# The second half of the last reload in four parts of rows, and a late correction moved from TensorE to VectorE

## The chip, the cores and the metric

The kernel runs on one core of a Trainium2 chip. The metric is the device time of one execution in microseconds (us), taken as the median of several timed runs. The profile comes from one further execution that the hardware profiler recorded.

## What is computed

The input `u` has 2048 tokens of 512 channels. A layer norm without weights gives `xn`. Two branches use it, and their results are added to the input:

```python
xn = (u - mean(u)) / sqrt(var(u) + 1e-5)                 # over the 512 channels
K  = Re(sum over 128 modes of C * exp(dt*A*l) * (dt*B))  # a filter of length 2048 for each channel
y  = irfft(rfft(pad(xn)) * rfft(pad(K)))[:2048] + xn * Dskip
h  = sigmoid(xn @ w_gate) * (xn @ w_up)                  # 512 -> 1792
out = u + y + h @ w_down                                 # 1792 -> 512
```

## The kernel before

**The two branches.** The gated branch runs in four groups of 512 tokens (`grp` 0 to 3). For each of 14 slices of 128 hidden columns TensorE computes the gate (L1045) and the up product (L1069), four matmuls each; ScalarE makes the sigmoid (L1057, L1060) and, for most slices, a copy of the up product (L1084); VectorE multiplies (L1089 from the copy, L1094 from PSUM). The down product (L1123) takes 14 matmuls of 512 columns for each tile of 128 tokens. The convolution branch is a Fourier transform over the tokens written as matmuls. It runs in two halves of 256 channels (`p` 0 and 1) with eight units `u` each. A unit transforms a slice (L885), brings the filter's spectrum to the same layout (L911), multiplies on VectorE (L916, L920), goes half the way back (L935), is copied to SBUF by ScalarE (L288) and stored to a scratch tensor `v_scr` in DRAM (L942). The last step of the way back mixes all units, so V is read again with the partition axis rearranged, and then multiplied with the constant `S2` (L994 in `s2_mm`).

**The reload.** `reload()` (L972) reads V back. The first half of the channels (`p` 0, `v0`) is four loads over all 128 partitions. The second half (`p` 1, `vall`) is cut by `VPART` (L409) into a part with six of the units, rows 0 to 95 of the scratch and partitions 32 to 127 of SBUF, and a part with the two units that are stored last, partitions 0 to 31. Each part is four loads `k`, one for each group of four output tiles, and each row of a load is two pieces of 2 KB (one for each `j`). `vall` has the order `[j, tile, channel]`.

**The tail.** Twelve of the sixteen output tiles have their gated result ready in SBUF early (`glu_sb`, with the input already added). For them `final(t)` (L999) runs `s2_mm` for a pair of tiles into one of two PSUM pairs, eight matmuls, and VectorE adds the gated result and writes the output tile (L1020, 1024 columns). The four tiles of group 3, tiles 12 to 15, are "late": TensorE sums the down product and the S2 product in one PSUM bank, and VectorE adds the input `xt` (L1143). The last of these is done in two halves of 256 columns. `xt` is a second load of tiles 12 to 15 of the input, issued on SP's queue late in the kernel (L1110), since the first copy was overwritten by the layer norm.

**The correction.** The way the input is laid out leaves out a few terms of the convolution for the last rows. Eight rows of corrections are computed from the first tokens (`pre`, L714) and two filter taps (`k2`, L950): five small VectorE operations make `rz` (L954 to L958), TensorE transposes it into PSUM (L964), ScalarE copies it to `rr` (L966), and in `s2_mm` one more matmul for each late tile (L997, 512 columns, or 256 in the halves) adds the right row through the selector `SR` (a constant, loaded at L852). `rr` is set to zero first by GpSimd (L854).

**What sets the order.** All work is recorded as operations of a `_Plan`. `ORDER` (L206) is a list of operation numbers, written out by hand, and the program is emitted in that order; so each engine's instruction order and each queue's order of DMAs is fixed. The slots of PSUM and of SBUF buffers are taken and returned in that same order. Most DMAs go through SP's queue, a few through ScalarE's and GpSimd's. The DMAs of SP and ScalarE take turns on eight semaphores, DMAHW0 to 7, so the issue of a DMA also waits until the DMA that had its semaphore before has landed.

Of the kernel before, what the change touches and what calls it, by code (L numbers as in the profile page):

```python
# [20 lines left out]
D = 512  # L21
# [38 lines left out]
PK = [42.24, 48.91]  # L60
SWD = (4, 6, 7)
# [121 lines left out]
def _consts():  # L183
# [16 lines left out]
    return dict(SR=f(sr), ident=f(np.eye(128)), S1=f(np.tile(S1, (4, 1))), S2=f(np.stack([_build_S2(by), np.roll(_build_S2(by), 32, axis=1)], axis=1)), M2=f(quads(M2[by])),  # L200
                MAB=f(np.stack([quads(MA[by], True), quads(MB[by], True)], axis=2)), E=f(_build_E(M2, by).reshape(128, NU // 2, 2, NKT, 128).transpose(1, 0, 2, 3, 4)))
# [117 lines left out]
def kernel(  # L319
# [75 lines left out]
    for nm, sz in [("W1", 12 * KB), ("gc", 2 * KB), ("G", 16 * KB), ("H", 20992), ("tmp", 4 * KB), ("W0", 12 * KB),  # L395
                   ("xn", 16 * KB), ("lad", 16 * KB), ("kx", 8 * KB), ("zs", 4 * KB), ("pq", 2 * KB)]:
        OFF[nm] = o
        o += sz
    s1 = at(OFF["kx"], [64])
    s2 = at(OFF["tmp"], [2, 64])  # L400
    rr = at(OFF["tmp"] + KB // 2, [D])
    sr = at(OFF["tmp"] + 3 * KB // 2, [4, 64])
    W = [at(OFF["W%d" % p], [12, 2, DW]) for p in range(NP)]
# [809 lines left out]
```

## Time and profile before

| | |
|---|---|
| three timed runs | 214.19, 215.49, 216.25 us; median 215.49 |
| profiled execution, its span from the first to the last instruction (no other time of it is given) | 213.6 us |
| TensorE (PE) busy | 204.2 us, 96% |
| VectorE (DVE) busy | 191.3 us, 90% |
| ScalarE (ACT) busy | 177.1 us, 83% |
| GpSimd (POOL) busy | 27.8 us, 13% |
| granted TensorE clock, mean | 1.000 |
| moved by DMA | 42.61 MB, mean 199 GB/s |

The rows that the prediction quotes are of these kinds. A row of the timeline has the start in us, the duration in us, the engine, the line, the operation, the tiles as out<-in, the shape, the count of merged instructions, and in brackets the idle time before it with what ended it. A name such as SPq is the sequencer of an engine that issues DMAs. A row of the windows has, for a stretch of time, the busy us and the number of instructions of PE, PEld (weight loads), DVE, ACT and POOL, then the granted clock, the mean busy share of the 16 DMA engines and what they moved in GB/s. Consecutive TensorE matmuls overlap, so the time that one costs is the distance between starts, which is shorter than its duration.

### The profile page before, as it was taken

The page shows a single profiled execution, that of the slowest core. Times are in us where ns is not written, and L with a number is a line of the kernel's source. Part 1 is how long each engine was busy: PE and PEld are TensorE (multiplying, and loading weights), DVE is VectorE, ACT ScalarE, POOL GpSimd, SP SyncE. Part 2 cuts the span into 40 slices and gives each one's busy share as a digit, 9 for nine tenths or more (in the row PEclk, how much of TensorE's full clock was granted, in tenths as well). Part 3 has the DMA queues.
Part 4 walks back from the last instruction along what each step waited for, and adds up shares of the span by engine and source line. Part 5 has one row for each costly group of instructions (what it writes and reads, how often), then busy time and mean ns, then how long its engine had stood idle before and what let it go on. Part 6 is the DMA issues. An engine that isn't in the chain of part 4 may idle for free.

```text
span 213.6 us, 4875 instructions
## 1 busy us (share of the span) xinstructions
PE 204.2 (96%) x1838; PEld 102.9 (48%) x1864; DVE 191.3 (90%) x406; ACT 177.1 (83%) x284; POOL 27.8 (13%) x32
## 2 busy tenths in 40 slices
PE   7989999999999999999999999999999999999992
PEld 2654444444443444445436555544654645644482
DVE  4799999999979999999999999999992999990494
ACT  5699999999999999997999989978989998870000
POOL 2120026008980000002000000001200000000000
PEclk9999999999999999999999999999999999999999
DMA  5999269124464236967965878787967799698864
GB/s 148 316 383 381 100 147 324 61 98 147 110 126 104 76 105 229 213 191 151 249 185 141 228 202 237 215 221 175 202 188 208 217 284 274 141 357 218 240 213 172
DMA packets 52377, 42.61 MB, mean 199 GB/s; under 512 B 16641, under 2 KB 44546, under 8 KB 52354
## 3 DMA queue, kind: packets, MB, share of 16 engines
q1 hardware_dynamic: 50658, 40.30, 63.9%
q0 software_dynamic: 864, 1.57, 4.8%
q10 hardware_dynamic: 832, 0.43, 0.8%
q8 instruction: 14, 0.23, 0.5%
q14 instruction: 9, 0.07, 0.1%
HBM read 24.99 MB, written 12.85 MB: 177 GB/s over the span
## 4 chain that ended last, share of the span: by engine, by line
PE 41%; DVE 40%; POOL 6%; DMA 4%; issue 4%; ACT 3%; DVEq 0%; SPq 0%; ACTq 0%
PE pair L911 8%; PE bank L1045 7%; PE bank L1123 7%; PE bank L1069 7%; DVE big L737 6%; DVE big L738 6%; POOL ln_ve_b L481 5%; PE pair L935 5%; DVE big L742 4%; DVE big L743 4%; DVE stats L542 3%; DVE hT_sb L1094 3%; DVE hT_sb L1089 3%; DVE big L678 2%; DMA big<-v_scr 2%
## 5 line engine op out<-in xcount | busy, mean ns | idle before, releaser
L288 ACT ACTIVATE big<-pair 128x1024 bf16<-128x1024 f32 x64 | 64.5, 1039 | 6.9 <-DVE big L920 1.7
L1069 PE MATMUL bank<-xnT,wu_sb 128*128 128x512 bf16 x214 | 52.9, 379 | 1.7 <-issue 0.6
L1123 PE MATMUL bank<-wd_sb,hT_sb 128*128 128x512 bf16 (+1 forms) x231 | 50.6, 367 | 0.5 <-issue 0.2
L1045 PE MATMUL bank<-xnT,wg_sb 128*128 128x512 bf16 (+1 forms) x191 | 45.6, 370 | 1.0 <-issue 0.5
L1045 PEld LDWEIGHTS <-wg_sb 128*128 128x128 bf16 x240 | 22.5, 98 | 25.0 <-issue 3.2
L1123 PEld LDWEIGHTS <-hT_sb 128*128 128x128 bf16 x238 | 22.4, 98 | 24.9 <-issue 1.6
L1069 PEld LDWEIGHTS <-wu_sb 128*128 128x128 bf16 x224 | 20.7, 98 | 27.5 <-issue 5.4
L1057 ACT ACTIVATE hT_sb<-bank 128x512 bf16<-128x512 f32 x48 | 28.2, 627 | 0.7 <-PE bank L1045 0.7
L737 DVE TENSOR_TENSOR big<-big 128x1024 bf16<-128x1024 bf16 (+4 forms) x40 | 26.7, 667 | 0.2
L738 DVE TENSOR_TENSOR big<-big 128x1024 bf16<-128x1024 bf16 (+4 forms) x40 | 26.5, 663 | 0.0
L1084 ACT ACTIVATE us_sb<-bank 128x512 bf16<-128x512 f32 x40 | 23.6, 616 | 0.6 <-DVE hT_sb L1089 0.3
L911 PE MATMUL pair<-big 128*128 128x256 bf16 x160 | 19.8, 273 | 0.0
L916 DVE TENSOR_TENSOR big<-big 128x2048 bf16<-128x2048 bf16 x16 | 19.3, 1217 | 0.1
L911 PEld LDWEIGHTS <-big 128*128 128x128 bf16 x160 | 15.4, 98 | 4.7 <-issue 0.8
L481 POOL TENSOR_SCALAR ln_ve_b<-mvb 128x4 bf16<-128x4 bf16 x3 | 13.0, 4323 | 34.1 <-DVE mvb L543 34.1
L742 DVE TENSOR_TENSOR big<-big 128x512 bf16<-128x512 bf16 (+4 forms) x40 | 16.5, 413 | 0.2
L743 DVE TENSOR_TENSOR big<-big 128x512 bf16<-128x512 bf16 (+4 forms) x40 | 16.5, 412 | 0.0
L792 ACT ACTIVATE sq_sb<-big 128x256 bf16<-128x256 bf16 (+2 forms) x20 | 13.2, 658 | 1.6 <-DVE big L743 1.5
L1089 DVE TENSOR_TENSOR hT_sb<-hT_sb,us_sb 128x1024 bf16<-128x1024 bf16 x20 | 13.5, 683 | 0.0
L935 PE MATMUL pair<-big 64*64 64x512 bf16 (+1 forms) x256 | 13.1, 327 | 0.0
L898 DVE COPY big<-big 32x1024 bf16<-32x1024 bf16 x20 | 8.4, 418 | 4.5 <-ACT big L288 4.2
L288 ACT ACTIVATE big<-big 128x256 bf16<-128x256 bf16 x30 | 12.4, 452 | 0.0
(99 smaller groups left out, 229.8 us busy)
## 6 DMA issues: line engine op xcount, KB each, us to landing
big<-c_E SPq DMA_DIRECT2D x13, 320.0 KB, 4.4
z_scr<-big SPq DMA_DIRECT2D x16, 256.0 KB, 2.9
big<-z_scr SPq DMA_DIRECT2D x16, 256.0 KB, 4.2
v_scr<-big SPq DMA_DIRECT2D x16, 256.0 KB, 3.2
big<-big SPq DMA_DIRECT2D x44, 64.0 KB, 3.3
big<-in_A_u_dram SPq DMA_DIRECT2D x4, 512.0 KB, 9.1
wu_sb<-in_B_w_up_dram SPq DMA_DIRECT2D x2, 896.0 KB, 10.8
wd_sb<-in_B_w_down_dram SPq DMA_DIRECT2D x1, 1792.0 KB, 9.0
```

Source lines behind the costliest of these rows:

```text
L288: nc.scalar.activation(out=get(out), in_=get(in_), func=ACT.Identity)
L481: P.tensor_scalar(out=q["ve_b"], in0=mvb[:, s, 1], scalar1=EPS, scalar2=None, op0=ALU.add)
L737: V.tensor_tensor(out=wide(outp), in0=wide(lo), in1=mre, op=ALU.mult)
L738: V.tensor_tensor(out=wide(tb()), in0=wide(lo), in1=mim, op=ALU.mult)
L742: V.tensor_tensor(out=outp[:, :, 0], in0=outp[:, :, 0], in1=tb()[:, :, 1], op=opr)
L743: V.tensor_tensor(out=outp[:, :, 1], in0=outp[:, :, 1], in1=tb()[:, :, 0], op=opi)
L911: T.matmul(two(sk)[:, o:o + DW], es()[:, g, kt, :], kTv[p][:, :, kt, :], start=kt in (0, NKT - 1), stop=kt >= NKT - 2)
L935: T.matmul(two(sv)[o:o + 64, DW * (2 * g + y):2 * DW * (g + 1)], mab[b:b + 64, 2 * u + g, q, :], pq()[b:b + 64, q, ch] if y else pp()[b:b ...
L1045: T.matmul(bank(sl, k % 2)[:, c0:c1], w[:, kt, k * 128:(k + 1) * 128], xnT[:, grp, kt, c0:c1], start=(kt == 0), stop=(kt == KT - 1))
L1057: S.activation(out=hT_sb[:, hs.idx, k % 2, :], in_=bank(sl), func=ACT.Sigmoid)
L1069: T.matmul(bank(sl), wu_sb[:, kt, k * 128:(k + 1) * 128], xnT[:, grp, kt, :], start=(kt == 0), stop=(kt == KT - 1))
L1123: T.matmul(bank(po)[:, 0:c[1] - c[0]], hT_sb[:, hts[k // 2].idx, k % 2, jj * 128:(jj + 1) * 128], wd_sb[:, k, c[0]:c[1]], start=first and ...
```

## The change

1. **The second half in four parts.** `VPART` cuts the second half by units 2-3, 4-5, 6-7 and 0-1. Each part has 32 rows, and these no longer go to neighbouring partitions: row `a` of part `b` goes to partition `4a + b`, so each part touches every fourth partition from end to end. The S2 constant for the second half has its rows rearranged to match, so `S2` is 64 KB, not 32.
2. **Longer pieces.** Columns of the constant `MAB` are reordered so that a row of V in the scratch has the order `[tile group, j, tile, channel]`, with tile groups in the order 0, 3, 1, 2 (`KORD`). The first three parts are then two loads each with one piece of 8 KB per row (256 KB a load; the first has tile groups 0 and 3, the second 1 and 2), and the last part is four loads with 4 KB pieces (128 KB each), two of them on ScalarE's queue as before. The loads of the first half have one piece of 4 KB per row.
3. **The last x tiles are kept.** Tiles 12 to 15 of the input are loaded to a tile `xt` of their own at the start, the layer norm reads them there and writes to `xn`, and the second load of 512 KB is gone.
4. **The correction on VectorE.** Two loads of 4 KB bring the eight input rows concerned next to the correction (`x8`). In the place of ScalarE's copy, VectorE adds the transposed correction to them (8x512), and two DMAs on ScalarE's queue write the eight sums over rows 95 and 127 of `xt`. The matmuls of L997, the load of `SR` (64 KB) and GpSimd's memset are gone.
5. **The order.** `ORDER` is new near the end.

```diff
-    sr = np.zeros((128, 4, 64))
-    for q in range(8):
-        sr[q, q // 2, 31 + 32 * ((q ^ (q // 2)) % 2)] = 1.0
...
+    MAB = MAB.reshape(MAB.shape[:3] + (2, 2, 4, 4)).swapaxes(4, 5)[..., KORD, :, :].reshape(MAB.shape)
+    spread = S2.reshape(4, 32, -1).swapaxes(0, 1)
...
-    VPART = ((0, 0, 8, 4), (1, 2, 8, 4), (1, 0, 2, 4))
+    VPART = ((0, 0, 8, 4), (1, 2, 4, 2), (1, 4, 6, 2), (1, 6, 8, 2), (1, 0, 2, 4))
...
-        ls = [load("SP", xn[:, i0:i0 + n, :], xv[:, i0:i0 + n, :], 128 * n * KB,
+        ls = [load("SP", xt[:] if i0 == 12 else xn[:, i0:i0 + n, :], xv[:, i0:i0 + n, :], 128 * n * KB,
...
-    l_sr = load("SP", sr, cten["SR"].ap(), 64 * KB, deps=table_free, pkt=512)
-    l_s2 = load("SP", s2, cten["S2"].ap(), 32 * KB, deps=table_free, pkt=256)
-    m_rr = pl.add("POOL", 0.3, lambda: P.memset(rr, 0.0), table_free, 60)
+    l_x8 = [load("SP", x8[b:8:2, :], xv[95 + 32 * b, 12:16, :], 4 * KB, deps=table_free, pkt=1024) for b in range(2)]
+    l_s2 = load("SP", s2, cten["S2"].ap(), 64 * KB, deps=table_free, pkt=512)
...
-    o_rz = pl.add("ACT", 0.48, lambda slr=slr: S.activation(out=rr[0:8, :], in_=bank(slr)[0:8, :], func=ACT.Identity), [o_rt, l_sr, m_rr], 60, rel=[slr])
-
-    vall = at(TAIL["vall"] + 16 * KB, [2, NT, DW])
+    o_rz = pl.add("DVE", 0.61, lambda slr=slr: V.tensor_tensor(out=rr[0:8, :], in0=bank(slr)[0:8, :], in1=x8[0:8, :], op=ALU.add), [o_rt] + l_x8, 60, rel=[slr])
+
+    vall = at(TAIL["vall"] + 16 * KB, [4, 2, 4, DW])
+    vspread = vall.rearrange("(a b) k j i d -> b a (k j i d)", b=4)
...
-                dst = v0[k][rows] if p == 0 else vall[rows, :, w * k:w * (k + 1)]
...
+                ks = KORD[w // 4 * k:w // 4 * (k + 1)]
+                cut = slice(2 * DW * w * k, 2 * DW * w * (k + 1))
+                dst = vspread[u0 // 2][:, cut] if p else v0[ks[0]].rearrange("p j i d -> p (j i d)")
...
-        if i >= 12:
-            T.matmul(o[64:128, :], sr[:, i - 12, :], rr[:, w[0]:w[1]], start=False, tile_position=(0, 64), **kw)
...
-                    xt = at(TAIL["xt"], [4, D])
-                    lx = [dma("SP", xt, xv[:, i:i + 4, :], deps=[prods[0]] + table_free, prio=3,
-                              pkt=4096)(512 * KB)]
+                    lx = [dma("ACT", xt[95 + 32 * b:96 + 32 * b, :, :], rr[b:8:2, :], deps=xn_ready[12:16] + [o_rz], prio=3, pkt=1024)(4 * KB) for b in range(2)]
...
-            ver = vp_op[i // 2] + [l_s2, o_rz]
+            ver = vp_op[i // 2] + [l_s2]
```

What the new order makes of the engines near the end is shown at three places. In these rows `pair_63` and `pair_64` are the two PSUM pairs, `bank_65` to `bank_68` the four banks, `big` is the large SBUF tile that holds most buffers, and brackets name the semaphores that an instruction waits for.

TensorE after its 28th matmul of the group-3 down products (L1123; L1129 in the changed kernel), where the first S2 products stand (L994; L1004). Rows that only repeat are left out. Before:

```order
L1123 MATMUL bank_67<-wd_sb,hT_sb 128x512
L994 MATMUL pair_64<-xnT,big 64x256 [waits DMAHW5_49]
L994 LDWEIGHTS big [waits DMAHW4_49]
L994 MATMUL pair_64<-big 64x256 [waits DMAHW2_49]
L994 MATMUL pair_63<-xnT,big 64x256 [waits Activation_49]
L1123 MATMUL bank_65<-wd_sb,hT_sb 128x512
```

Changed:

```order
L1129 MATMUL bank_66<-wd_sb,hT_sb 128x512
L1004 LDWEIGHTS big [waits DMAHW4_49]
L1004 MATMUL bank_66<-big 64x256 [waits DMAHW4_49]
L1004 LDWEIGHTS big [waits DMAHW5_49,DMAHW4_49,DMAHW3_49]
L1004 MATMUL bank_66<-big 64x256 [waits DMAHW0_49]
L1004 MATMUL bank_68<-big 64x256
L1004 MATMUL pair_64<-xnT,big 64x256 [waits DMAHW6_49]
L1004 MATMUL pair_64<-big 64x256 [waits DMAHW0_49]
```

Eight S2 matmuls of the first two late tiles (banks 66 and 68) now stand ahead of the first two finals; before they stood, with a matmul of L997 each, behind the third down product in bank 65. So the first S2 matmul now needs tile group 3 of all four parts, and the finals behind it need group 0.

VectorE from its last product of the gated branch to the end. L1020 and L1143 are L1028 and L1149 in the changed kernel. Before:

```order
L1094 TENSOR_TENSOR hT_sb<-hT_sb,bank_66 128x512
L1020 TENSOR_TENSOR big<-pair_64,glu_sb 128x1024
L1020 TENSOR_TENSOR big<-pair_63,glu_sb 128x1024
L1143 TENSOR_TENSOR big<-bank_68,big 128x512
L1143 TENSOR_TENSOR big<-bank_67,big 128x512
L1143 TENSOR_TENSOR big<-bank_65,big 128x512
L1020 TENSOR_TENSOR big<-pair_64,glu_sb 128x1024
```

Changed:

```order
L1102 TENSOR_TENSOR hT_sb<-hT_sb,bank_67 128x512
L973 TENSOR_TENSOR big<-pair_63,big 8x512
L1028 TENSOR_TENSOR big<-pair_64,glu_sb 128x1024
L1028 TENSOR_TENSOR big<-pair_63,glu_sb 128x1024
L1149 TENSOR_TENSOR big<-bank_68,xt 128x512
L1149 TENSOR_TENSOR big<-bank_66,xt 128x512
L1149 TENSOR_TENSOR big<-bank_65,xt 128x512
L1028 TENSOR_TENSOR big<-pair_64,glu_sb 128x1024
```

The order of kinds is the same, and the addition of the correction (L973) has come in ahead of the first final. What differs is when the banks of the first two late tiles are ready, by the rows of TensorE above.

SP's queue around the last stores of V. Before, `v_scr_100` is the part with six units and `v_scr_101` that with the last two:

```order
L422 DMA big<-in_A_u_dram 128x2048 [waits DMAHW3_49]
L422 DMA v_scr_101<-big 128x4x256 [waits DMAHW0_49,Activation_49]
L422 DMA v_scr_101<-big 128x4x256 [waits DMAHW1_49,Activation_49]
L422 DMA big<-v_scr_100 96x2x1024 [waits DMAHW4_49,DMAHW6_49,DMAHW2_49,DVE_49]
L422 DMA big<-v_scr_101 32x2x1024 [waits DMAHW1_49,DMAHW0_49]
L422 DMA big<-v_scr_100 96x2x1024 [waits DVE_49]
```

Changed, where `v_scr_101`, `_102` and `_103` are the parts of units 2-3, 4-5 and 6-7, and `v_scr_104` that of the last two units:

```order
L430 DMA v_scr_101<-big 128x4x256 [waits DMAHW7_49,Activation_49]
L430 DMA big<-v_scr_102 32x4096 [waits DMAHW1_49,DMAHW3_49,DMAHW0_49,DVE_49]
L430 DMA v_scr_104<-big 128x4x256 [waits Activation_49]
L430 DMA v_scr_104<-big 128x4x256 [waits DMAHW2_49,Activation_49]
L430 DMA big<-v_scr_103 32x4096
L430 DMA big<-v_scr_101 32x4096 [waits DMAHW7_49,DMAHW5_49]
L430 DMA big<-v_scr_104 32x2048 [waits DMAHW2_49,DMAHW1_49,DMAHW0_49]
L430 DMA big<-v_scr_104 32x2048 [waits DVE_49]
L430 DMA big<-v_scr_102 32x4096 [waits DMAHW3_49,DVE_49]
```

One load of the second half now stands ahead of the last two stores, two stand between them and the load that waits for them, and the load of the input is gone. On ScalarE's queue stand, in this order, two loads of `v_scr_104` and the two DMAs from the correction to `xt`. On ScalarE itself two copies of the up product (L1084) now stand ahead of the copy that the sixth unit's store waits for, and on TensorE a group of four up matmuls has changed places with the four gate matmuls next to it.

More of the change, by code (lines that the diff above doesn't have):

```diff
@@ L540, in layernorm @@
                 continue
-            b_s = pl.add("DVE", 0.6, lambda i=i: V.bn_stats(out=stats[:, i, :], in_=xn[:, i, :]), l_x[i], prio)
+            b_s = pl.add("DVE", 0.6, lambda i=i: V.bn_stats(out=stats[:, i, :], in_=x_in(i)), l_x[i], prio)
             st.append(pl.add("DVE", 0.1, lambda i=i: V.bn_aggr(out=mvb[:, i, :], in_=stats[:, i, :]), [b_s], prio - 0.001))
@@ L548, in fa @@
                 def fa(i=i):
[L549 removed]
+                    S.activation(out=xn[:, i, :], in_=x_in(i), func=ACT.Identity, scale=lnt["ri_f"][:, i:i + 1],
                                  bias=lnt["nb_f"][:, i:i + 1])
@@ L973, in reload @@
         for n, (p, u0, u1, nt) in enumerate(VPART):
[L974 to L975 removed]
+            v_v = v_scr[n][:].rearrange("g q d -> (g q) d").rearrange("(p kc) d -> p (kc d)", kc=32)
             for k in range(nt):
                 w = NT // nt
[L978 to L983 removed]
+                ks = KORD[w // 4 * k:w // 4 * (k + 1)]
+                cut = slice(2 * DW * w * k, 2 * DW * w * (k + 1))
+                dst = vspread[u0 // 2][:, cut] if p else v0[ks[0]].rearrange("p j i d -> p (j i d)")
+                free = x_use[ks[0]] + ([o_pre] if ks[0] == 0 else []) if p == 0 and ks[0] < 3 else table_free if p == 0 else table_free + x_done
+                ld = dma("ACT" if n == 4 and k % 2 else "SP", dst, v_v[:, cut], deps=v_st[n] + free, prio=20 + n + 0.02 * k,
+                         pkt=1024 * w, hv=0.9)(16 * KB * w * (u1 - u0))
+                for kk in ks:
+                    vp_op[2 * kk].append(ld)
+                    vp_op[2 * kk + 1].append(ld)
     def glu_at(i):
```

38 lines of the change are left out of this document (18 added, 20 removed), and 82 rows, old and new, of the table ORDER.

## Prediction

> **What bounds the kernel now.** I read the stages first (the windows), then each engine's timeline in the last stages, then the landings of the DMAs that feed them.
>
> ```profile
> 165.00:182.00 17.00, 16.50 (x163) 9.75 (x168) 16.58 (x28) 15.43 (x18) 0.00 (x0) 1.00 0.88 252
> 182.00:192.00 10.00, 9.79 (x103) 5.33 (x98) 9.90 (x20) 7.88 (x10) 0.00 (x0) 1.00 0.82 254
> 192.00:198.10 6.10, 6.10 (x31) 2.60 (x30) 0.73 (x2) 0.59 (x1) 0.00 (x0) 1.00 0.86 228
> 198.10:202.60 4.50, 4.06 (x30) 2.07 (x30) 2.36 (x2) 0.00 (x0) 0.00 (x0) 1.00 0.84 223
> 202.60:206.90 4.30, 4.30 (x52) 3.64 (x51) 3.56 (x5) 0.00 (x0) 0.00 (x0) 1.00 0.69 233
> 206.90:210.50 3.60, 2.96 (x33) 2.11 (x30) 3.57 (x5) 0.00 (x0) 0.00 (x0) 1.00 0.62 228
> ```
>
> Up to 192 us both TensorE (9.79 of 10.00) and VectorE (9.90 of 10.00) are full: an edit there gains little unless it removes work from both. From 192 to 198.1 only TensorE works (6.10 of 6.10) and VectorE has nothing to do. From 202.6 on VectorE is nearly full again. So the tail goes from TensorE to VectorE, and the question is where it changes hands.
>
> ```profile
> 191.94 6.22 PE L1123 MATMUL bank<-wd_sb,hT_sb 128*128 128x512 bf16 x28
> 198.09 0.30 PE L994 MATMUL pair<-xnT,big 128*64 128x256 bf16 x2
> 198.67 0.30 PE L994 MATMUL pair<-big 128*64 128x256 bf16 x2 [0.28 <-DMA big<-v_scr]
> 198.80 0.28 PE L994 MATMUL pair<-xnT,big 128*64 128x256 bf16 x2
> 199.35 0.28 PE L994 MATMUL pair<-big 128*64 128x256 bf16 x2
> 199.78 2.97 PE L1123 MATMUL bank<-wd_sb,hT_sb 128*128 128x512 bf16 x13 [0.16 <-issue]
> 202.68 0.51 PE L994 MATMUL bank<-big 128*64 128x256 bf16 x5
> 205.21 0.27 PE L994 MATMUL pair<-big 128*64 128x256 bf16 x1
> 199.23 2.36 DVE L1020 TENSOR_TENSOR big<-pair,glu_sb 128x1024 bf16<-128x1024 f32 x2 [6.50 <-PE pair L994]
> 203.34 1.94 DVE L1143 TENSOR_TENSOR big<-bank,big 128x512 bf16<-128x512 f32 x3 [1.76 <-PE bank L997]
> 205.20 2.34 DVE L1020 TENSOR_TENSOR big<-pair,glu_sb 128x1024 bf16<-128x1024 f32 x2
> 207.47 0.41 DVE L1143 TENSOR_TENSOR big<-bank,big 128x256 bf16<-128x256 f32 x1
> 207.80 2.34 DVE L1020 TENSOR_TENSOR big<-pair,big 128x1024 bf16<-128x1024 f32 x2
> 210.06 0.41 DVE L1143 TENSOR_TENSOR big<-bank,big 128x256 bf16<-128x256 f32 x1
> 210.14 0.33 DVEq L1209
> ```
>
> Three things are to be seen. TensorE reaches the first S2 product at 198.09 and its second pair, due one step of 0.11 us later (198.80 to 199.35 are five steps), starts at 198.67: it lost 0.47 us to a load of V. VectorE idles 1.76 us before the first late addition at 203.34, because that tile's S2 and correction matmuls stand behind the third down product. And from 203.34 to the end at 210.47 VectorE never stops: 7.13 us, so the end is VectorE's. After that come 3.1 us of output DMA and closing, which the change leaves as they are.
>
> **The change, part by part.** *Order of the tail.* With the S2 products of late tiles 12 and 13 ahead of the finals, both banks are complete before VectorE ends its two finals. First S2 at 198.09 without a wait; four steps for the banks (0.44), then the eight steps of the two finals. The first final's last step starts at 198.09 + 7 x 0.11 = 198.86, and VectorE starts 0.32 later (199.23 less 198.91, one step after 198.80) at 199.18, as before. Two finals at 1.13 (half of 205.20 to 207.47) and two late additions at 0.62 (a third of 203.34 to 205.20) end at 202.7. The third late tile: before, its first S2 step came at 202.68, which is 4.12 after 198.09 when the 0.47 are taken out; now 198.09 + 0.44 + 4.12 = 202.65, second step 202.76, ready at 203.08. From there VectorE has one late addition, four finals and two halves, all continuous: 7.13 - 2 x 0.62 = 5.89, so it ends at 208.97 and not 210.47. **Gain 1.50 us**: 1.24 from two additions that move into the idle time, 0.26 from the block's earlier start.
>
> *The matmuls of L997.* From 202.68 to 205.21 there are 15 steps of 0.11 (1.65) and the five correction matmuls: 2.53 - 1.65 = 0.88 us of TensorE. It is not added to the sum: they stood in front of VectorE's block only through the first of them. But it is what keeps TensorE ahead afterwards. Its next steps are: two finals and the half bank from 202.87 to 203.85, 256-column down products until 205.3 (like 205.42 to 207.05), finals 205.5 to 206.5 (the second waits for its PSUM pair until about 206.0), down products until 208.2. VectorE wants those results at 203.7, 204.8, 205.9, 206.3, 207.4 and 208.6; each is there by 0.1 us or more. If this cover were gone, 0.88 would come back behind 203.08.
>
> *The loads of V.* This decides whether the 198.09 stands.
>
> ```profile
> 191.27 2.59 DMA v_scr<-big
> 193.92 4.70 DMA big<-v_scr
> big<-v_scr SPq DMA_DIRECT2D x4, 384.0 KB, 7.0
> big<-v_scr ACTq DMA_DIRECT2D x2, 128.0 KB, 5.2
> DMA to landing us min/median/max: 2.5/4.3/7.2
> big<-in_A_u_dram SPq DMA_DIRECT2D x4, 128.0 KB, 2.2
> 188.00:190.00 2.00, 2.00 (x35) 1.02 (x34) 2.00 (x5) 1.02 (x2) 0.00 (x0) 1.00 1.08 383
> 194.00:195.00 1.00, 1.00 (x7) 0.41 (x5) 0.00 (x0) 0.00 (x0) 0.00 (x0) 1.00 0.70 219
> 195.00:196.00 1.00, 1.00 (x6) 0.46 (x5) 0.00 (x0) 0.00 (x0) 0.00 (x0) 1.00 0.70 201
> ```
>
> The last store is issued at 191.27 and lands 2.59 us later, 193.86; no load of the last two units can go before, in either kernel. Before, that load took 4.70 us for 128 KB, behind 384 KB, while loads of 96 and 32 neighbouring partitions moved 201 to 219 GB/s with engines idle (share 0.70); with loads over all 128 partitions in flight the DMAs reached 383 GB/s (188 to 190). No row shows a load of 32 rows set four apart. Bounds for its landing after an issue at 193.94: 2.2 us (the row of 128 KB alone) gives 196.1; 7.2, the slowest load of V, gives 201.1. Between them: what is still to move for the first S2 step when stores end, about 193.2, is two loads of 256 KB and two of 128 KB, 786 kB, at 210 GB/s 3.7 us, so 196.9, some 197.5 with the other two 128 KB loads beside it. I take 197.2, 0.9 us before 198.09, so the wait is 0; it costs nothing only while the 28 down products (6.1 us) run over it. The later halves are issued by 197 and wanted at 202.9, with 3 us to spare even at 2.5 to 3 us each.
>
> [...]
>
> *What is removed from SP and DMA.*
>
> ```profile
> 182.41 1.42 SPq L422 DMA_DIRECT2D big<-in_A_u_dram  x1
> 190.35 1.27 SPq L422 DMA_DIRECT2D v_scr<-big  x2
> 165.21 0.55 SPq L422 DMA_DIRECT2D big<-c_SR  x1
> 165.80 1.93 SPq L422 DMA_DIRECT2D big<-big  x3
> 172.03 1.23 DVE L916 TENSOR_TENSOR big<-big 128x2048 bf16<-128x2048 bf16 x1
> ```
>
> The 512 KB input load with its 1.42 us of SP's queue goes; two loads of V's first half move up by that much, out of the way of the last stores. Nothing on the path waits there, so 0; at most the 0.21 us that TensorE is not busy between 182 and 192, and the 0.50 of the stage before. The one load of `SR` becomes two small ones, another 0.6 us of queue ahead of three swaps of a unit. The last of them was issued at about 167.1 and is read by the product at 172.03, so even with the median 3.3 us of such swaps there is room for 0.6.
>
> *VectorE and ScalarE before the tail.*
>
> ```profile
> 189.26 1.28 DVE L1089 TENSOR_TENSOR hT_sb<-hT_sb,us_sb 128x1024 bf16<-128x1024 bf16 x2
> 190.47 0.17 DVE L954 TENSOR_TENSOR rf<-pre,k 128x16 f32<-128x16 f32 x1
> 191.62 0.39 PE L964 MATMUL pair<-ident,rz 128*8 128x128 bf16 x4
> big<-big SPq DMA_DIRECT2D x44, 64.0 KB, 3.3
> ```
>
> One product of 0.60 now stands before the five small operations, which then end at about 191.6, where the transpose at 191.62 waits for them: up to 0.1 later for TensorE and all behind it; I take **0.05 loss**. The addition of the correction (8x512 from PSUM, by the nearest row 0.62) runs at about 192.8 to 193.5, in the 6.5 us that VectorE idles; without that cover it would cost 0.62. Its two DMAs to `xt` are third and fourth on ScalarE's queue, issued by 196; by 2.2 to 5.2 us they land between 198 and 201.2, and the first late addition starts at 201.4. The two copies of ScalarE that move ahead delay the sixth unit's store by 1.1 us, to about 188; it is not among the last two, and the loads of its part go after 191.6. I take 0 for both.
>
> The sum: 1.50 - 0.05 = 1.45 us. Span 213.6 becomes 212.15. The runs' median of 215.49 lies 1.9 above the span, and the same distance gives **214.0 us**, 0.7% faster. About 1% (2.15 us) is what a measurement of this kernel can tell from no change; the three runs lie 2.06 apart.
>
> **The rivals.** *Slower: the wait at the first S2 step.* This step now needs group 3 of all parts, the last of it from ScalarE's queue, and twice the bytes of the second half before it. Every us that this lands after 198.1 is added to the end. With 7.2 us it lands at 201.1: 3.0 us of wait against 1.45 of gain, 217.0 us. It decides from a landing at 199.6. For it: two landings near 7 us in the same place. Against it: those loads queued behind up to 0.9 MB, and the pending bytes are fewer now. Chance 0.12.
>
> *The wait stays as it was.* The last load takes 4.7 to 5.2 us as in the old rows and lands at 198.6 to 199.1, a wait of 0.5 to 1.0: 214.8. Chance 0.17.
>
> *The early relief counts.* The freed queue closes TensorE's gaps of 0.21 and 0.50 us: 213.3. Against it: those gaps end with "issue" or VectorE, not DMA. Chance 0.10.
>
> *The change does not do what it says.* If the eight sums reach `xt` only at about 203, behind the loads on ScalarE's queue, the first two late additions find the banks complete but not the input, and the idle time stays: 215.3. Chance 0.06.
>
> **How the numbers follow.** The forecast has 0.55. Of it 0.17 falls beyond 1% by the spread of the runs; with 0.07 of the third rival and 0.03 of the second, faster has 0.27. Of the first rival 0.06 is beyond +1% (a landing after 201.7, or 217.0 and some spread), and 0.02 of the rest: slower 0.08. The remaining 0.65 is within 1%. The range 212.3 to 216.3 reaches from 1.7 below, the spread and the third rival, to between the last rivals and the first.
>
> **What would show it.** Right: no L997; the first S2 matmul at 198.1 to 198.2 and no DMA wait in the eight steps; VectorE's two late additions start at 201.4 directly behind the two finals, with 0.3 to 0.4 of idle ahead of the third; VectorE ends near 209.0; the last 128 KB loads land in 3 to 3.5 us. Wrong: a wait for `big<-v_scr` or for `xt<-big` of over 0.5 us, VectorE idle after 203.1, or TensorE starting its 28 matmuls later than 192.1.

## The result, and the profile after

The changed kernel takes **213.69 us** (median of 20 runs, 212.38 to 214.69); the kernel before took 215.1 in 20 runs beside it (213.74 to 217.49). The ratio is 0.9933, 95% interval 0.9908 to 0.9957: 0.7% faster, within the 1% that was called no change. The forecast was 214.0 against 215.49, a ratio of 0.9931.

The stages of the changed kernel, in windows cut at its own hand-overs (first TensorE's 28 down products alone, then the tail):

```profile
182.80:192.80 10.00, 9.79 (x105) 5.31 (x98) 9.90 (x20) 7.89 (x11) 0.00 (x0) 1.00 0.78 232
192.80:198.90 6.10, 6.10 (x29) 2.62 (x28) 1.35 (x3) 0.00 (x0) 0.00 (x0) 1.00 0.87 262
198.90:203.40 4.50, 4.34 (x38) 2.52 (x38) 3.38 (x4) 0.00 (x0) 0.00 (x0) 1.00 0.61 199
203.40:207.70 4.30, 4.30 (x57) 3.47 (x57) 3.94 (x6) 0.00 (x0) 0.00 (x0) 1.00 0.55 202
207.70:209.80 2.10, 1.54 (x14) 1.13 (x12) 2.10 (x3) 0.00 (x0) 0.00 (x0) 1.00 0.76 271
```

Up to 192.8 nothing changed (TensorE 9.79 of 10.00, VectorE 9.90, as before). In the third row VectorE is busy for 3.38 us where the matching stage of before had 2.36.

The whole of this execution runs 0.83 us behind the one of before, from its start: VectorE waited about that much longer for the first input tiles, which both kernels load in the same way. The first fence is from VectorE's timeline before, the second from that of the changed kernel; the bracket is the wait for the load.

```profile
2.92 1.29 DVE L542 BATCH_NORM_STATS2 stats<-big 128x6 f32<-128x512 bf16 x2 [2.92 <-DMA big<-in_A_u_dram]
4.61 0.69 DVE L542 BATCH_NORM_STATS2 stats<-big 128x6 f32<-128x512 bf16 x1
```

```profile
3.48 1.28 DVE L550 BATCH_NORM_STATS2 stats<-big 128x6 f32<-128x512 bf16 x2 [3.48 <-DMA big<-in_A_u_dram]
5.62 0.69 DVE L550 BATCH_NORM_STATS2 stats<-big 128x6 f32<-128x512 bf16 x1 [0.36 <-DMA big<-in_A_u_dram]
```

The third tile came 1.01 us later (5.62 less 4.61), and 0.83 of it is still there at the first down product (192.77 against 191.94). The change is not the reason: in the runs below that load the input as the changed kernel does, the first down product starts anywhere from 190.82 (e10) to 192.47 (e7). So the spans (212.7 and 213.6) differ by less than the tails do. I compare **tails** from here on: from the start of the first of the 28 down products to the end of VectorE's last addition. Before, that was 191.94 to 210.47 = 18.53 us. After, from the timelines of TensorE and VectorE:

```profile
192.45 0.39 PE L971 MATMUL pair<-ident,rz 128*8 128x128 bf16 x4
192.77 6.22 PE L1129 MATMUL bank<-wd_sb,hT_sb 128*128 128x512 bf16 x28
198.91 0.63 PE L1004 MATMUL bank<-big 128*64 128x256 bf16 x8
203.47 0.41 PE L1004 MATMUL bank<-big 128*64 128x256 bf16 x4
207.54 1.70 PE L1129 MATMUL bank<-wd_sb,hT_sb 128*128 128x256 bf16 x14
193.47 0.67 DVE L973 TENSOR_TENSOR big<-pair,big 8x512 bf16<-8x512 f32 x1
200.02 2.36 DVE L1028 TENSOR_TENSOR big<-pair,glu_sb 128x1024 bf16<-128x1024 f32 x2 [5.87 <-PE pair L1004]
202.29 1.28 DVE L1149 TENSOR_TENSOR big<-bank,xt 128x512 bf16<-128x512 f32 x2
203.93 0.69 DVE L1149 TENSOR_TENSOR big<-bank,xt 128x512 bf16<-128x512 f32 x1 [0.35 <-PE bank L1004]
204.53 2.34 DVE L1028 TENSOR_TENSOR big<-pair,glu_sb 128x1024 bf16<-128x1024 f32 x2
206.79 0.41 DVE L1149 TENSOR_TENSOR big<-bank,xt 128x256 bf16<-128x256 f32 x1
207.13 2.34 DVE L1028 TENSOR_TENSOR big<-pair,big 128x1024 bf16<-128x1024 f32 x2
209.39 0.41 DVE L1149 TENSOR_TENSOR big<-bank,xt 128x256 bf16<-128x256 f32 x1
```

192.77 to 209.80 is **17.03 us, 1.50 less than before**. The eight S2 matmuls of tiles 12 and 13 start at 198.91 as one unbroken group; no wait stands in brackets. The two late additions (202.29) follow the two finals directly, where VectorE idled 1.76 us before.

TensorE waits for no load and no other engine there either. Its last down product before ended here:

```profile
208.16 1.70 PE L1123 MATMUL bank<-wd_sb,hT_sb 128*128 128x256 bf16 x14
```

That is 209.86, or 17.92 after its first; now it is 209.24, or 16.47 after. TensorE's part of the tail became 1.45 us shorter: the lost 0.47, the five matmuls' 0.88, and a rest of 0.10. VectorE's last addition follows it by 0.2 and 0.15 us in the two kernels. Two chains thus end almost together in both, and this decides the experiments.

### The profile page after: what moved, and what is told of

It reads as the page before. It is cut to its first block, busy times and chain, and to the rows that moved or that the text cites. A ratio compares the mean times of both kernels' runs of the same rounds, so it can differ in the third digit from the quotient of the medians.

```text
span 212.7 us, 4875 instructions
## 1 busy us (share of the span) xinstructions
PE 202.0 (95%) x1833; PEld 101.8 (48%) x1859; DVE 191.8 (90%) x407; ACT 176.4 (83%) x283; POOL 27.4 (13%) x31
## 4 chain that ended last, share of the span: by engine, by line
PE 42%; DVE 40%; POOL 6%; ACT 5%; issue 3%; DMA 2%; SPq 1%; ACTq 0%; DVEq 0%
PE bank L1129 10%; PE pair L918 8%; PE bank L1077 7%; PE bank L1053 6%; DVE big L745 6%; DVE big L746 6%; POOL ln_ve_b L489 5%; PE pair L942 5%; DVE big L750 4%; DVE big L751 4%; DVE hT_sb L1102 3%; DVE stats L550 3%; DVE hT_sb L1097 3%; ACT big L292 2%; DVE big L686 2%
## 5 line engine op out<-in xcount | busy, mean ns | idle before, releaser
L1129 PE MATMUL bank<-wd_sb,hT_sb 128*128 128x512 bf16 (+1 forms) x231 | 50.6, 366 | 0.5 <-issue 0.2
L1129 PEld LDWEIGHTS <-hT_sb 128*128 128x128 bf16 x238 | 22.5, 98 | 24.9 <-issue 1.6
L489 POOL TENSOR_SCALAR ln_ve_b<-mvb 128x4 bf16<-128x4 bf16 x3 | 12.2, 4081 | 33.9 <-DVE mvb L551 33.9
```

The lines of the kernel that those rows point to most:

```text
L1129: T.matmul(bank(po)[:, 0:c[1] - c[0]], hT_sb[:, hts[k // 2].idx, k % 2, jj * 128:(jj + 1) * 128], wd_sb[:, k, c[0]:c[1]], start=first and ...
```

## The experiments

Each edit is made to the changed kernel unless said otherwise. The tails are worked out as above, each from one profiled execution (the changed kernel and e5, which does the same work and one more load, have the same 17.03); the wait is what the second of the first S2 steps comes later than one step (0.11) after the first, and the ratio is to the kernel before, with its interval.

| run | wait at first S2, us | tail, us | ratio |
|---|---|---|---|
| kernel before | 0.47 | 18.53 | 1 |
| changed kernel | 0 | 17.03 | 0.9933 [0.9908, 0.9957] |
| S2 of late tiles back (e1) | 0 | 17.79 | 0.9992 [0.9968, 1.0016] |
| five matmuls back (e4) | 0 | 17.80 | 0.9989 [0.9968, 1.0010] |
| input load back (e5) | 0 | 17.03 | 0.9931 [0.9904, 0.9958] |
| old parts (e3) | 3.11 | 21.49 | 1.0132 [1.0082, 1.0183] |
| old parts, 8 KB pieces (e10) | 2.52 | 21.18 | 1.0041 [1.0009, 1.0072] |
| old parts, groups 1 and 2 late (e11) | 1.70 | 26.17 | 1.0350 [1.0320, 1.0381] |
| neighbouring rows (e2) | 0 | 17.13 | 0.9943 [0.9909, 0.9976] |
| 4 KB pieces (e7) | 0 | 17.53 | 0.9954 [0.9921, 0.9987] |
| both of these (e12) | 0 | 17.74 | 0.9929 [0.9906, 0.9952] |
| 1 MB of loads ahead (e6) | 1.53 | 19.99 | 1.0099 [1.0064, 1.0135] |

**The order undone (e1).** The numbers are positions of operations in `ORDER`; 912 and 915 are the S2 products of tiles 12 and 13, 834 and 831 the first finals', 918 the third down product.

```diff
-    825, 828, 821, 827, 830, 915, 912, 602, 834, 831, 918, 919
+    825, 828, 821, 827, 830, 602, 834, 831, 918, 912, 915, 919
```

> The changed kernel with one thing undone: TensorE's S2 products of the late tiles 12 and 13 stand again behind the third down product. Measure: the tail, from the first of the 28 down products to VectorE's last operation (before 18.53 us, changed 17.03). Theory, the order is the gain: VectorE idles some 1.4 us again ahead of its first late addition, whose operands are then complete 4.4 us after the first S2 step, and the block of 7.1 us follows; tail 17.9, time 0.9 us above the changed kernel, ratio to the kernel before 0.997. Rival, the removed wait and the five removed matmuls are the gain and the order is not: tail 17.0 to 17.2, ratio 0.993.

Measured: tail 17.79, 0.76 more than the changed kernel (0.9 was expected). VectorE in this run:

```profile
198.91 2.36 DVE L1028 TENSOR_TENSOR big<-pair,glu_sb 128x1024 bf16<-128x1024 f32 x2 [5.53 <-PE pair L1004]
202.81 1.89 DVE L1149 TENSOR_TENSOR big<-bank,xt 128x512 bf16<-128x512 f32 x3 [1.55 <-PE bank L1004]
204.61 2.34 DVE L1028 TENSOR_TENSOR big<-pair,glu_sb 128x1024 bf16<-128x1024 f32 x2
...
209.47 0.41 DVE L1149 TENSOR_TENSOR big<-bank,xt 128x256 bf16<-128x256 f32 x1
```

The idle time is back (1.55), and behind it VectorE's block is whole again: 202.81 to 209.88, 7.07 us. By the tails the order is worth 0.76, and the rest of the change, the new reload and the absent matmuls, brings 0.74 without it (18.53 less 17.79). The timed runs leave less for the rest: without the order the ratio cannot be told from 1, though its interval reaches down to 0.9968, 0.69 us.

**Five matmuls put back (e4).** They multiply a tile of zeros.

```diff
+        if i >= 12:
+            T.matmul(o[64:128, :], s2[:, 0, 0, :], zero[:, w[0]:w[1]], start=False, tile_position=(0, 64), **kw)
```

> The changed kernel with five matmuls put back where the correction matmuls stood (behind the S2 products of each late tile, two of 256 columns and three of 512, on a tile of zeros, so that they add nothing). Theory, TensorE has no gap from the first down product to its last, so each of them is paid in full: 0.88 us less the 0.15 by which TensorE's last product leads VectorE's last addition; tail 17.7 to 17.9, ratio 0.9965. Rival, VectorE alone sets the end: only the three ahead of the third late addition count, 0.66 us less the 0.35 that VectorE idles there; tail 17.3, ratio 0.995. Second rival, they lie in other waits and cost nothing: tail 17.0.

Measured: tail 17.80, 0.77 more, within the 17.7 to 17.9 of the first theory. The ends of TensorE and VectorE:

```profile
191.25 6.22 PE L1133 MATMUL bank<-wd_sb,hT_sb 128*128 128x512 bf16 x28
206.89 1.70 PE L1133 MATMUL bank<-wd_sb,hT_sb 128*128 128x256 bf16 x14
208.63 0.42 DVE L1153 TENSOR_TENSOR big<-bank,xt 128x256 bf16<-128x256 f32 x1
```

TensorE's last product ends 17.34 after the first down product (206.89 + 1.70 less 191.25), 0.87 later than without them: all five are paid in full. By the tails e1 and e4 each take back half of the 1.50, though their causes are on different engines. (By the ratios each takes back 1.2 to 1.3 us, with intervals wide enough to hold 0.76.) That is what two chains of nearly equal length do: either alone, made longer, sets the end.

**The order alone (e8, e9).** This is the kernel before with its operations 909 and 912 (S2 and correction of tiles 12 and 13) moved ahead of the finals.

```diff
-    911, 825, 832, 833, 829, 828, 824, 826, 915, 909, 921, 822, 823, 830, 831, 827, 912, 916
+    911, 825, 912, 909, 832, 833, 829, 828, 824, 826, 915, 921, 822, 823, 830, 831, 827, 916
```

> The kernel before with one part of the change alone: TensorE's S2 products and correction matmuls of the late tiles 12 and 13 moved ahead of the first finals; loads, corrections and parts as before. Theory, the order is not to be had without the new loads and without the removed matmuls: those products now come 0.88 us ahead of the finals and want group 3 of V, whose second load was issued at 194.58 and would land near 200; wait 1 to 2 us in place of 0.47, and the end is TensorE's; tail 18.5 to 19.8, ratio 1.000 to 1.006. Rival, the order alone takes VectorE's two additions into its idle time and gains by itself: tail 17.3 to 17.9, ratio 0.994 to 0.997.

Here I made a mistake. 828 and 824 load group 3, and in the program they now stand behind the products that read it. So those products took what lay in the buffer (tiles 12 and 13 of this run are computed from old rows of V), and the loads waited for them:

```profile
199.01 1.47 ACTq L422 DMA_DIRECT2D big<-v_scr  x2
```

In the kernel before, the first of these two was issued at 194.01. The ratio, 1.0119 [1.0081, 1.0157], is that of loads 5 us late and says nothing on the order. The next run has the loads ahead of the products:

```diff
-    911, 825, 832, 833, 829, 828, 824, 826, 915, 909
+    911, 825, 828, 824, 912, 909, 832, 833, 829, 826, 915
```

> The kernel before with the order alone: the S2 products and correction matmuls of late tiles 12 and 13 ahead of the first finals, and the two loads of group 3 that they read put ahead of them (in the run before this one the loads stood behind the products, so those read old rows and the loads waited for them). Theory, the order is not to be had without the new loads: group 3's second load, issued near 194, lands like the others of that queue (4.7 to 5.6 us) at 198.6 to 199.7, and two correction matmuls stand ahead of the finals; the wait is 0.5 to 1.6 us at the first S2 step, and TensorE's whole tail is as long as before or longer: tail 18.3 to 19.8, ratio 0.999 to 1.006. Rival, the order alone takes two of VectorE's additions into its idle time and gains by itself: tail 17.3 to 17.9, ratio 0.994 to 0.997.

Measured: ratio 1.0106 [1.0069, 1.0143], 2.3 us slower than before and above the range expected. Its one profiled execution took 219.91, 1.8 above the median of its twelve, so I read no length from it, only the place: TensorE waits for `big<-v_scr` at the first S2 step. The rival, a gain from the order alone, is excluded. With the old loads, though two of them were moved ahead, the order costs time.

**The old parts (e3).**

```diff
-    VPART = ((0, 0, 8, 4), (1, 2, 4, 2), (1, 4, 6, 2), (1, 6, 8, 2), (1, 0, 2, 4))
+    VPART = ((0, 0, 8, 4), (1, 2, 8, 4), (1, 0, 2, 4))
-                dst = vspread[u0 // 2][:, cut] if p else v0[ks[0]].rearrange("p j i d -> p (j i d)")
+                dst = vall.rearrange("p k j i d -> p (k j i d)")[16 * u0:16 * u1, cut] if p else v0[ks[0]].rearrange("p j i d -> p (j i d)")
```

The rows of S2's constant follow, and the loads stand in `ORDER` where the loads of the four parts stood.

> The changed kernel with the second half of V stored and reloaded as before: parts of six units and of two, on neighbouring partitions, 4 KB pieces; the order of the tail, the kept x and VectorE's correction stay. Theory, the new order can only stand because the new parts land in time: the first S2 step, which now wants group 3, waits 0.5 to 2 us for it, tail 17.5 to 19.0, ratio 0.9955 to 1.003. Rival, the freed queue and the fewer bytes are enough for the old parts too: wait under 0.2 us, tail 17.0 to 17.2, ratio 0.993.

Measured: a wait of 3.11 us and a tail of 21.49. Wait, tail and ratio are all above the ranges expected, and the tail grew by 4.46, 1.35 more than the wait. The chain of waits (start, duration, what) and then the windows of this run:

```profile
193.26 7.40 DMA big<-v_scr
200.66 0.04 issue
200.71 0.85 PE bank L1004 x3
201.55 1.71 PE pair L1004 x11
```

```profile
197.60:200.70 3.10, 0.19 (x2) 0.00 (x0) 0.00 (x0) 0.00 (x0) 0.00 (x0) 0.92 1.02 194
200.70:203.00 2.30, 2.29 (x22) 1.78 (x22) 0.55 (x1) 0.00 (x0) 0.00 (x0) 0.50 0.48 125
203.00:204.00 1.00, 0.67 (x6) 0.34 (x4) 1.00 (x2) 0.00 (x0) 0.00 (x0) 0.70 0.02 8
```

The load took 7.40 us against 3.9 in the changed kernel, while the DMA engines were full (share 1.02) at only 194 GB/s. The second and third windows have the extra 1.35: after 3.1 us without work the granted clock is 0.50, and steps of 0.11 take 0.21 (pair products start at 201.35 and 201.56). With a clock of 1.00 or 0.50 throughout, a mean of 0.92 over the 3.10 us before and of 0.70 over the last window put the half clock from 200.2 to 203.6, 3.4 us, of which TensorE had work in the last 2.9.

**What of the reload matters (e2, e7, e12, e10, e11).** The change gave it three properties: finer parts, rows set apart, longer pieces. First the rows alone (e2), with the `dst` of e3 and S2's rows not rearranged:

```diff
-    spread = S2.reshape(4, 32, -1).swapaxes(0, 1)
+    spread = S2
```

> The changed kernel with the 32 rows of each part of V's second half on neighbouring partitions in place of every fourth; pieces of 8 KB, number of loads and order stay. Theory, the rows' places set the speed of a load: with each load on a quarter of the partitions the last of them lands 1.5 to 3 us later, the first S2 step waits 1 to 2.5 us, and above about 3 us of wait the granted clock falls to 0.5 as in the run with the old parts; tail 18.0 to 21.0, ratio 0.998 to 1.012. Rival, the pieces and the number of issues set it: no wait, tail 17.0 to 17.3, ratio 0.993.

The rival holds: no wait, tail 17.13. But the rows are not without effect. The 3.1 us before the first S2 step, first of e2 and then of the changed kernel:

```profile
194.99:198.09 3.10, 3.10 (x15) 1.27 (x13) 0.00 (x0) 0.00 (x0) 0.00 (x0) 1.00 1.01 202
```

```profile
195.77:198.87 3.10, 3.10 (x15) 1.27 (x13) 0.00 (x0) 0.00 (x0) 0.00 (x0) 1.00 0.76 245
```

Neighbouring rows keep the engines busy for 1.01 of the time to move 202 GB/s; rows set apart move 245 in 0.76. Per full engine time that is 200 against 322 GB/s. The loads landed after 3.9 to 4.5 us, not 3.5 to 4.4. In e2 the last two that the first S2 step needs went at 193.87 and 193.88 and took up to 4.3 us, to 198.2, just when that step started (198.14). The margin of half a us is used up, 0.2 of it by a later issue, counted from the first down product, and the rest by the slower landing.

Then the pieces alone (e7):

```diff
-    VPART = ((0, 0, 8, 4), (1, 2, 4, 2), (1, 4, 6, 2), (1, 6, 8, 2), (1, 0, 2, 4))
+    VPART = ((0, 0, 8, 4), (1, 2, 4, 4), (1, 4, 6, 4), (1, 6, 8, 4), (1, 0, 2, 4))
```

> The changed kernel with pieces of 4 KB in place of 8: each of the three parts of units two to seven is reloaded in four loads of 128 KB, not two of 256, so six issues more; rows set four apart as in the change. Theory, the rows' places set the speed: the wait at the first S2 step is at most 0.3 us (0.6 us of queue for one issue more ahead of the last load, against a margin of 0.5), tail 17.0 to 17.4, ratio 0.993 to 0.995. Rival, the long pieces set it: wait 1 to 3 us, tail 18 to 21, ratio 0.998 to 1.012.

No wait at the first S2 step, as the theory had it; the tail of 17.53 is a little above its range, by a wait that neither theory had, at the third pair of tiles, which reads the later groups (0.48 by the rule of the table, 0.32 of it idle):

```profile
204.01 0.30 PE L1004 MATMUL pair<-big 128*64 128x256 bf16 x2 [0.32 <-DMA big<-v_scr]
```

Both together (e12, the edits of e2 and e7), so that only the finer parts are left:

> The changed kernel with both neighbouring rows and pieces of 4 KB, so that of the new reload only its four parts of two units are left (against the run with the old parts, nothing but the parts and the place of their loads differs). Theory, the fine parts carry the reload: two of them can start before the last stores, and each holds back less; the first S2 step waits under 0.5 us, and a wait of 0.5 to 1 us for the second halves appears later as with the short pieces; tail 17.5 to 18.3, ratio 0.995 to 1.000. Rival, one of the other two is needed beside the parts: a wait of 1 to 3 us at the first S2 step, tail 18.5 to 21.5, ratio above 1.000.

Tail 17.74, in the theory's range, with 0.69 us of wait at the third pair and none at the first S2 step, where all eight matmuls are one group:

```profile
198.18 0.63 PE L1004 MATMUL bank<-big 128*64 128x256 bf16 x8
```

(The ratio, 0.9929 with an interval to 0.9952, is lower than this tail would give, some 0.996; it was six runs, and I go by the profile.) **The finer parts, with the places in the queue that they allow, carry the first S2 step**; rows and pieces each add a margin, the pieces probably by sparing six issues ahead of the later groups (a median of 0.57 us an issue in e7), which was not tried apart. Two more runs ask why parts of six units are slow. With longer pieces (e10, from e3):

```diff
-    VPART = ((0, 0, 8, 4), (1, 2, 8, 4), (1, 0, 2, 4))
+    VPART = ((0, 0, 8, 4), (1, 2, 8, 2), (1, 0, 2, 4))
```

> The run with the old parts (first S2 step waits 3.1 us there), with pieces of 8 KB in place of 4: the part of six units is loaded in two loads of 768 KB, groups 0 and 3 together first, then 1 and 2 together. Theory, sizes of pieces do not matter and the parts of six units do (all their bytes can only start after 191.2, and groups 1 and 2 share the engines with what is wanted first): the first S2 step waits 2.3 to 3.3 us, tail 20.5 to 21.8. Rival, the short pieces were the slow thing: wait under 1 us, tail 17.0 to 18.0.

The wait and the clock behind it:

```profile
199.59 0.52 PE L1004 MATMUL bank<-big 128*64 128x256 bf16 x6 [2.33 <-DMA big<-v_scr]
```

```profile
199.60:200.10 0.50, 0.50 (x10) 0.50 (x12) 0.00 (x0) 0.00 (x0) 0.00 (x0) 1.00 1.15 295
200.10:202.00 1.90, 1.90 (x20) 1.12 (x15) 1.19 (x2) 0.00 (x0) 0.00 (x0) 0.52 0.38 91
```

The wait is 2.52 and the tail 21.18, in the theory's ranges; the wait is 0.6 us shorter than in e3. The tail grew by 1.63 more than the wait. The mean of 0.52 puts the fall to 0.50 at 200.2, and TensorE's weight loads start some 0.43 us apart up to 203.64 and some 0.2 apart from there:

```profile
202.81 0.15 PEld L1129 LDWEIGHTS <-hT_sb 128*128 128x128 bf16 x1 [0.28 <-issue]
203.24 0.15 PEld L1129 LDWEIGHTS <-hT_sb 128*128 128x128 bf16 x1 [0.28 <-issue]
203.64 1.61 PEld L1129 LDWEIGHTS <-hT_sb 128*128 128x128 bf16 x8 [0.25 <-issue]
```

So the clock was 0.50 for some 3.4 us again, here all of it under work, and this execution paid more than e3 for a shorter wait. It is not so in every execution: four of the ten timed runs, this one among them, have a mean granted clock of 0.988 to 0.990 and took 216.91 to 218.44; the other six have 0.996 or more and took 214.57 to 216.92, and the ratio of 1.0041 would go with a tail of some 19.4. And with the loads of groups 1 and 2 (823, 824, 827, 828) put behind the first output (834), again from e3:

```diff
-    833, 827, 823, 830, 908, 907, 911, 914, 918, 824, 835, 836, 834, 920
+    833, 830, 908, 907, 911, 914, 918, 835, 836, 834, 823, 824, 827, 828, 920
```

> The run with the old parts (first S2 step waits 3.1 us there), with one thing different: the loads of groups 1 and 2, which the first S2 step does not read, stand behind the first output store on SP's queue and behind the sums to xt on ScalarE's. Theory, the wait came from loads that nobody needs yet and that shared the DMA engines with group 3's: the first S2 step waits under 1.2 us, TensorE keeps its full clock, and the delayed groups cost a second wait later (at the last finals) of 1 to 3 us. Rival, the parts of six units are slow by themselves: the first wait stays at 2.5 to 3.3 us.

```profile
199.18 0.52 PE L1004 MATMUL bank<-big 128*64 128x256 bf16 x6 [1.51 <-DMA big<-v_scr]
```

The first wait is 1.70, between the two ranges, so neither theory holds whole: of 3.11 us, 1.4 came from loads that nobody needed yet. (Tiles 4 and 5 stand ahead of their load here and take old rows; from there on this run is only a series of late loads, and its total is not used.) For the other 1.70 I have an explanation that I only argue: in e3 nothing of group 3 can start before 191.2, while in the changed kernel the first 256 KB were issued at 189.23, ahead of the last two stores.

**The input load back (e5).**

```diff
+    xd = at(8 * KB, [4, D])
+    dma("SP", xd, xv[:, 12:16, :], deps=[pl.ops[520]] + table_free, prio=3, pkt=4096)(512 * KB)
```

> The changed kernel with the 512 KB input load put back on SP's queue, at the place where the kernel before issued it, to room that the late tiles' input had; nobody reads it. Theory, the removed load gained nothing: tail 17.0 to 17.2, TensorE's gaps of the stage before 192 as they are, ratio 0.993. Rival, the relief of the queue and the DMA counts: V's first loads move back by 1.4 us and the first S2 step waits or TensorE's gaps grow, 0.3 to 0.7 us, ratio 0.9945 to 0.9965.

Tail 17.03, ratio 0.9931: those 512 KB cost nothing. But the load was issued some 6 us earlier than in the kernel before, counted from the first down product, and took 0.34 us of queue in place of 1.42:

```profile
176.17 0.34 SPq L430 DMA_DIRECT2D big<-in_A_u_dram  x1
```

So this tests its bytes, not its former place in the queue.

**A late landing priced (e6).** Two loads of 512 KB behind the part 825 on SP's queue. They overwrite a part of the tail's buffers, so some output is computed from wrong data; the work is the same.

```diff
+    for n in range(2):
+        xd = at((8 + 4 * n) * KB, [4, D])
+        dma("SP", xd, xv[:, 12:16, :], deps=table_free, prio=3, pkt=4096)(512 * KB)
```

> The changed kernel with 1 MB of loads that nobody reads (two of 512 KB, to free room) put on SP's queue ahead of the last two parts of V's second half. It prices a late landing. At 260 to 380 GB/s these bytes take 2.8 to 4.0 us, against a margin of 0.5 at the first S2 step: a wait of 2.3 to 3.5 us. Theory, each us of wait is added to the end and a wait near 3 us costs another 1.3 by the clock: tail 19.3 to 21.9, ratio 1.004 to 1.016. Rival, the wait is partly taken back since VectorE idles ahead of its third late addition and TensorE's later work has slack: tail 17.5 to 19.0.

The wait is 1.53 and not 2.3 to 3.5. The tail grew by 2.96, in the theory's range but by another sum: 1.53 at the first S2 step, and a second wait of 1.3 at the third pair, whose loads moved back too. VectorE's idle time ahead of its third late addition stayed 0.36, so it took nothing back. In this execution TensorE kept its clock:

```profile
199.20:201.00 1.80, 1.56 (x23) 1.31 (x25) 0.60 (x1) 0.00 (x0) 0.00 (x0) 1.00 0.30 76
```

Two of the other six timed runs have a mean clock of 0.989 and 0.991, as low as in e3 (0.992); no profile shows where they lost it.

## Why the prediction was right, point by point

**The order, 1.50.** Right in size: the tail is 1.50 shorter, and VectorE's first late addition came directly behind the finals, with 0.35 us idle ahead of the third (0.3 to 0.4 was said). The reason was told one-sidedly. The sum put 1.24 and 0.26 down to VectorE's order alone, with the five matmuls at nothing beside it but named as the cover, 0.88 if it were gone. e4 shows the cover (0.77), e1 the order (0.76), and e9 that the order without the rest costs. What each engine needed for the same 1.5 us was a different part of the change: VectorE the order, TensorE the absent matmuls and the absent wait. A sum on one engine gave the right end because the other had 0.1 to 0.15 to spare (0.15 by the rows above, 0.11 by e4: 0.88 less 0.77); the prediction's list of TensorE's next steps had that, with "0.1 us or more".

**The loads of V, no wait.** Right, with a smaller margin. I took a landing 0.9 us ahead of the first S2 step. The last two loads that it needs, one on each queue:

```profile
194.47 1.38 ACTq L430 DMA_DIRECT2D big<-v_scr  x2
194.47 2.01 SPq L430 DMA_DIRECT2D big<-v_scr  x3
DMA to landing us min/median/max: 3.8/3.9/3.9
```

Issued at 194.47 and 3.9 us under way, they landed at 198.4, 0.5 ahead of 198.91. The issue came 0.3 earlier than the estimate on the shifted clock (194.77), the transfer took some 0.6 longer than 3.26. The sign "in 3 to 3.5 us" was thus missed: these loads took 3.8 to 3.9.

**The later halves, "3 us to spare".** Wrong, without effect on the result. They were to be issued by 197:

```profile
198.43 1.09 SPq L430 DMA_DIRECT2D big<-v_scr  x2
DMA to landing us min/median/max: 4.3/4.3/4.4
```

They went at 198.43 and 198.93 and landed by 203.3, 0.4 us before the pair that reads them at 203.72. The later issue is not a queue's length: SP's queue waits 1.9 us here until a load of V has landed, and 198.43 is directly behind the landing (198.41) of ScalarE's load of 194.47, whose semaphore, one of eight, it has in the trace. If e11 holds here too, this even helps, as it keeps 512 KB out of the way of the first S2 step; that was not tried apart. By e7 it is the next thing to give: six issues more make it a wait.

**The rows' places.** The 210 GB/s of the prediction came from loads on neighbouring rows; no row of before had rows set four apart. e2 shows a difference: 32 neighbouring rows needed more engine time for the same bytes, 200 against 322 GB/s above. What makes it was not measured. The tail shows little of it, 17.13 us against 17.03.

**What was costed at nothing.** The input load: 0 (e5). The small correction chain: 0.05 was taken for a later transpose, and it started at 192.45, 0.83 behind before, so 0.00. The 28 down products started at 192.77, past the 192.1 that the prediction had named as a sign of being wrong; on the shifted clock that is 191.94, as before. VectorE's addition of eight rows ran at 193.47 for 0.67, inside its idle time. The two DMAs to `xt` went out by 197.3, and no addition waited for them, so the rival of a late `xt` did not come about. The early relief of SP's queue brought nothing: TensorE's 9.79 of 10.00 is unchanged.

**The slower rival.** It did not come about; its price was too low. "Every us is added to the end" held in the profiled executions of e6 (1.53 us of wait) and, as far as the clock goes, of e11 (1.70; clock 1.00 behind the first wait), but not in those with longer ones. At 2.52 us (e10) the clock fell half a us after work resumed (0.52 in that window), at 3.11 (e3) it was 0.50 at once; e10 paid 1.63 on top and e3 1.35. The "about 3 us" in the expectation of e2 is thus no limit: in the profiled execution of e10 2.52 us was enough, and three more of its ten runs have as low a mean clock (0.988 to 0.990). With e3's 1.35, the rival's 3.0 us of wait would have cost about 4.35, and the time would have been 218.4, not 217.0: an estimate from e3's tail.

What stays open: why e3's wait is 1.70 with the competing loads away, of which only the later start of the first 256 KB was argued. No run takes back the two copies of ScalarE that moved ahead or TensorE's exchanged groups; no gain or loss is seen in their stage, where TensorE and VectorE are as busy as before.

## What to carry to other kernels

Where two engines end a stage almost together, make both sums to the end, and put each part of a change to the engine that it relieves: here the parts are worth 1.5 us together, undoing either takes back half, and one of them alone (e9) cost time. When a reload sits between the last store and its first use, cut it along the stores, so that most of it can go before the last one (no wait in e12, 3.11 us in e3), and keep what is not needed yet out of the engines (1.4 of the 3.11 us, e11). Price a long wait of TensorE above its length: in the traced executions 2.52 us cost 1.63 more (e10) and 3.11 us 1.35 more (e3), with the clock halved for some 3.4 us behind either.

## What the runs showed that I had not expected

The start of two executions differed by 0.83 us through input loads that are the same in both kernels, as much as half of the effect; the tail, compared from its own start, was 17.03 in the changed kernel and in e5, which began it 1.30 us apart. Rows set apart cost the issuing queue more, per load, than neighbouring ones (min/median/max in ns of the changed kernel, then of e2), which no term of the prediction had:

```profile
L430 SPq DMA_DIRECT2D big<-v_scr x8: 448/525/592, 189.2 to 198.9; - x8
```

```profile
L430 SPq DMA_DIRECT2D big<-v_scr x8: 302/370/547, 188.5 to 198.5; - x8
```

And in e11 the clock of TensorE, once fallen, was not back as soon as work resumed: behind a wait of 6 us later in the run its mean was 0.56 over 3.4 us, which is 0.50 for 3.0 us, until 213.6, and 14 matmuls took 2.77 us in place of 1.70.

```profile
210.55 0.43 PE L1004 MATMUL pair<-big 128*64 128x256 bf16 x2 [5.86 <-DMA big<-v_scr]
211.34 2.77 PE L1129 MATMUL bank<-wd_sb,hT_sb 128*128 128x256 bf16 x14
214.04 0.30 PE L1004 MATMUL pair<-xnT,big 128*64 128x256 bf16 x2
```

```profile
204.50:210.50 6.00, 0.19 (x4) 0.00 (x0) 1.40 (x2) 0.00 (x0) 0.00 (x0) 0.69 0.83 234
210.60:214.00 3.40, 3.40 (x20) 2.16 (x20) 1.23 (x1) 0.00 (x0) 0.00 (x0) 0.56 0.45 167
214.00:215.00 1.00, 1.00 (x19) 0.91 (x18) 0.72 (x2) 0.00 (x0) 0.00 (x0) 1.00 0.23 86
```
